# Gated linear attention with a segment memory: key sums of both signs on 128 lanes, denominators inverted once, k weights on a second queue, a new order

## The chip, the cores and the metric

One core of one Trainium2 chip runs the whole kernel. The metric is device time of the program in microseconds (us), lower is better. The engines are TensorE (PE), VectorE (DVE), ScalarE (ACT), GpSimd (POOL) and SyncE (SP); SP only issues DMAs here.

## The reference

The input x has 2048 tokens of 640 numbers, in bf16. Two attentions with 32 heads of 20 numbers each share it, and a gate mixes them:

```
# A: linear attention with softmax features of both signs
q, k, v = split(x @ wqkv)
phi(u)  = concat(softmax(u @ w_phi), softmax(-(u @ w_phi)))   # per head, 40 features
kv = sum over tokens of phi(k) x v ;  z = sum over tokens of phi(k)
o  = (phi(q) @ kv) / (phi(q) @ z + 1e-6);   a = o @ wo
# B: four segments of 512 tokens
per segment: causal softmax attention inside it (a_dot), and a read of a memory M, z (a_mem)
             o = g*a_mem + (1-g)*a_dot;  then M += phi(k) x v, z += sum phi(k)
b = o @ wo_B
out = s*a + (1-s)*b,   s = sigmoid(sum(x * gate_w))
```

## The kernel before

A graph of some 1,380 operations is written down in Python (`setup`, `b_proj`, `b_pair`, `b_out`, `b_mem`, `b_ret`, `a_k`, `a_kv`, `a_fin`, `a_q`, `final`). Three tables, found by a search, fix the rest: `ORDER` lists the operations by number in the order in which each engine's and each queue's instructions are written, `ENGINE` has one digit for each operation that may run on more than one engine, `PLACE` gives each buffer its slot in SBUF or its PSUM banks. An engine runs its instructions in that order and waits on semaphores. SP's DMAs are a queue of the same kind: a DMA that waits for data holds up the ones behind it.

What the change touches:

- `setup` loads x, transposed, and the weights. B's q and k weights come in six pieces each (`stq`, `stk`; L390) and are copied into a padded layout (`WB`, L448).
- `b_out(n)` works on segment n of B. The weighted values and the sums of weights lie in DRAM (`scn`), 32 heads x 21 rows. Four DMAs (`nB<-scn`) bring them back with lanes for features, the sum of each head repeated over its lanes; DVE inverts the sums (`nrec`, L714), and a multiply by them follows (`nmul`, L716).
- `a_k(t)` takes 128 tokens: two exponentials of k @ w_phi with scale +1 and -1 (`kexp`, L738) go to the two planes of the tile E, `Zred` and `Zrec` make the softmax sums, `Anorm` (L748) divides.
- `a_kv(S)` takes four such tiles. On PE, `kv` (L765) multiplies E with v, for each plane with all 128 lanes. For z, the four tiles are added up in a chain into `acc` (`chain`, L787): first on 64 lanes, then a DMA (`accmv`, acc<-acc) moves the sums to the other 64 lanes, and the chain goes on there, for each plane by itself. So it takes 16 adds of 64 lanes x 640 for each S.
- `a_fin` turns `acc` into lanes (L799) and builds `K1` (L809 and L811), the table for the queries; `a_q` and `final` use it. `final(t)` does the output projection of 128 tokens, 20 matmuls (L905), one eviction (`out_ev`, through `evac`, L399 on ACT, L400 on DVE), one DMA.
- A PSUM tile that spans two banks is read with one instruction (`pbanks`).

Of the kernel before, what the change touches and what calls it, by code (L numbers as in the profile page):

```python
# [13 lines left out]
D = 640  # L14
# [21 lines left out]
class Op:  # L36
    __slots__ = ("name", "engs", "fn", "writes", "deps", "tiles", "stream", "idx", "dma", "inc", "key", "val", "vc", "extra", "pos", "part")
# [42 lines left out]
class Graph:  # L80
# [6 lines left out]
    def op(self, engs, name, fn, R=(), W=(), after=(), dma=False, part=128):  # L87
# [17 lines left out]
        o.extra = []  # L105
        self.ops.append(o)
# [49 lines left out]
    def emit(self):  # L156
# [10 lines left out]
        for o in self.order:  # L167
            ds = dict.fromkeys(o.deps)
            if o.stream == "pool" and not o.dma:

                if last is not None and last.part != o.part:
                    ds[last] = None
                last = o
            for t in o.tiles:
                if t in o.writes:
                    for d in t.prev:
                        ds[d] = None
            o.extra = [d for d in ds if d is not o]
            for d in o.extra:
                if not (d.stream == "pe" and o.stream == "pe" and not d.dma):  # L180
                    d.inc = True
# [22 lines left out]
        for o in self.order:  # L204
            st = o.stream
            kn = known[st]
            need = [d for d in o.extra if not (d.stream == "pe" and st == "pe" and not d.dma)]
# [37 lines left out]
class GatedMix(Graph):  # L245
# [34 lines left out]
    def memory(self):  # L280
# [37 lines left out]
        self.onec = fx("onec", [128, 1], BF16)  # L318
# [18 lines left out]
        self.p_z = self.pool("z", 256, 4)  # L337
        self.p_r = self.pool("r", 128, 6)
# [12 lines left out]
        self.scq = [Tile(f"scq{i}", None, None, None) for i in range(2)]  # L351
        for i in range(2):
            self.scr[i].t = nc.dram_tensor(f"scr{i}", [240, 2, LSEG], BF16, kind="Internal").ap()
            self.scn[i].t = nc.dram_tensor(f"scn{i}", [NG, 128, LSEG], BF16, kind="Internal").ap()
            self.scq[i].t = nc.dram_tensor(f"scq{i}", [D, LSEG], BF16, kind="Internal").ap()
# [21 lines left out]
    def pbanks(self, t, n):  # L377

        a = t.t[0]
        assert len(t.t) == 2 and t.t[1] == a + 1  # L380
        return self.ps[:, 512 * a:512 * (a + 2)].rearrange("p (b c) -> p b c", b=2)[:, :, 0:n]
# [23 lines left out]
    def setup(self):  # L405
# [5 lines left out]
        for k in range(2):  # L411
            sl = slice(256 * k, 256 * k + 256)
            self.dma("sp", "x0", xT[:, :, sl], x2d[sl, :], W=[(xT, (0, k))], transpose=True)
        for l, (a, b) in enumerate(((0, 1), (1, 3), (3, NCH))):
            for nm, st in (("B_wq", self.stq), ("B_wk", self.stk)):
                for k, c0, c1 in ((0, 80 * a, 80 * b), (1, 400 + 48 * a, 400 + 48 * b)):
                    self.dma("sp", f"st{k}", st[:, :, c0:c1], wsrc(ins[nm])[:, :, c0:c1], W=[(st, (k, l))], noncontig=True)
        self.dma("sp", "WvB", self.WvB[:, :, 0:D], wsrc(ins["B_wv"]), W=[(self.WvB, "w")])
# [40 lines left out]
        op("dve", "ms", lambda e: e.memset(self.onec[:, :], 1.0), W=[(self.onec, "*")])  # L459
# [23 lines left out]
        bc = lambda a, n: a.rearrange("p (h o) -> p h o", o=1).to_broadcast([128, 4, n])  # L483
        for c in range(NCH):
            gs = lambda j, c=c: eb[:, 2, 4 * c:4 * c + 4] if j == 0 else eb[:, 2, 20 + XH[c]:24 + XH[c]]
            ms = lambda j, c=c: Mg[:, :] if j == 0 else Mx[:, c, XH[c]:XH[c] + 4]
            for j in range(2):
                R = [(eb, "*")] + ([(Mg, "*")] if j == 0 else [(Mx, i) for i in range(4)])
                op("dve", "Mm", lambda e, c=c, j=j, gs=gs, ms=ms: e.tensor_tensor(
                    Mm[:, c, 4 * j:4 * j + 4, 0:DH], bc(ms(j), DH), bc(gs(j), DH), ALU.mult), R=R, W=[(Mm, (c, j, 0))])  # L490
                op("dve", "Mm1", lambda e, c=c, j=j, ms=ms: e.tensor_copy(Mm[:, c, 4 * j:4 * j + 4, DH], ms(j)), R=R, W=[(Mm, (c, j, 1))])
# [87 lines left out]
    def b_mem(self, n):  # L579
# [6 lines left out]
        for b, cs in ((0, (0, 1, 2)), (1, (3, 4))):  # L586
# [16 lines left out]
            else:  # L603
# [3 lines left out]
                R=[(self.M32, b)] + [(self.Mm, (c, j, k)) for c in cs for j in range(2) for k in range(2)], W=[(self.Mz[n % 2], b)])  # L607
# [96 lines left out]
    def b_out(self, n):  # L704

        nB = self.nB[n]
        for dd in range(4):
            self.dma("sp", "nr", lambda dd=dd: nB[32 * dd:32 * dd + 32, :, :],
                     self.scn[n % 2].t.rearrange("g (i r) t -> r (g i) t", r=32)[dd:dd + 24:4].rearrange("c h t -> h c t"),
                     R=[(self.scn[n % 2], "*")], W=[(nB, ("r", dd))])  # L710
        w = 128 if n == 3 else 256
        for q in range(0, LSEG, w):
            qs = list(range(q // 128, (q + w) // 128))
            self.op("dve", "nrec", lambda e, q=q: e.reciprocal(nB[:, NCH, q:q + w], nB[:, NCH, q:q + w]),  # L714
                    R=[(nB, ("r", dd)) for dd in range(4)], W=[(nB, ("d", q))])
            self.op(("dve", "pool"), "nmul", lambda e, q=q: e.tensor_tensor(  # L716
                nB[:, 0:NCH, q:q + w], nB[:, 0:NCH, q:q + w], nB[:, NCH, q:q + w].rearrange("p (o t) -> p o t", o=1).to_broadcast([128, NCH, w]), ALU.mult),
                R=[(nB, ("d", q))] + [(nB, ("r", dd)) for dd in range(4)], W=[(nB, x) for x in qs])
# [11 lines left out]
    def a_k(self, t):  # L730
# [5 lines left out]
        self.op("pe", "pkA", self.tok_proj(pt, t, self.WkA), R=[(self.WkA, ic) for ic in range(NCH)] + self.xk(t), W=[(pt, 0)])  # L736
        for s in range(2):
            self.op("act", "kexp", lambda e, s=s: e.activation(E[:, s, :].rearrange("p (b c) -> p b c", b=2), self.pbanks(pt, 320), ACT.Exp, scale=1.0 - 2.0 * s),  # L738
                    W=[(pt, 0), (E, s)])
# [13 lines left out]
    def a_kv(self, S):  # L753
        ts = [4 * S + i for i in range(4)]
        for s in range(2):
            for b, cs in ((0, (0, 1, 2)), (1, (3, 4))):
                pt = self.pst("kv", 1)
                h0, h1 = CO[cs[0]], (CO + (NHC,))[cs[-1] + 1]

                def mm(e, s=s, pt=pt, cs=cs, h0=h0):  # L760
                    first = True
                    for c in cs:
                        lo, hi = HEADS_OF[c]
                        for t in ts:
                            r = e.matmul(self.pf(pt, 0, DH * (CO[c] - h0), DH * (hi - lo + 1)), lhsT=self.Et[t][:, s, 128 * c:128 * (c + 1)],  # L765
                                         rhs=self.vt[t][:, DH * lo:DH * (hi + 1)], start=first, stop=True, skip_group_check=True)
                            first = False
                    return r
                self.op("pe", f"kv{b}", mm, R=[(self.Et[t], s) for t in ts] + [(self.vt[t], "*") for t in ts], W=[(pt, 0)])
                dst = self.KVa[:, s, h0:h1, :].rearrange("p h d -> p (h d)")  # L770
                src = lambda pt=pt, n=DH * (h1 - h0): self.pf(pt, 0, 0, n)
# [4 lines left out]
        acc = self.acc  # L776
        a, b = (0, 1) if S % 2 == 0 else (1, 0)
        for s in range(2):
            def half(hf, first):
                lo = 64 * hf  # L780
                for k, t in enumerate(ts):
                    src = lambda t=t, s=s, lo=lo: self.Et[t][lo:lo + 64, s, :]
                    R = [(self.Et[t], s)]
                    if first and k == 0:
                        self.op(("dve", "pool"), "chain0", lambda e, src=src, s=s, lo=lo: e.tensor_copy(acc[lo:lo + 64, s, :], src()), R=R, W=[(acc, (hf, s))], part=64 + hf)
                    else:
                        self.op(("dve", "pool"), "chain", lambda e, src=src, s=s, lo=lo: e.tensor_tensor(acc[lo:lo + 64, s, :], acc[lo:lo + 64, s, :], src(), ALU.add),  # L787
                                R=R, W=[(acc, (hf, s))], part=64 + hf)
# [263 lines left out]
```

## Time and profile before

| | |
|---|---|
| median of 3 runs | 303.97 us (302.23 to 304.0) |
| profiled execution, its own time | 304.66 us |
| its span, first to last instruction | 302.9 us |
| granted TensorE clock, mean | 0.994 |
| PE busy | 273.9 us (90%), 2991 matmuls |
| DVE busy | 239.1 us (79%), 407 instructions |
| ACT busy | 242.3 us (80%), 282 |
| POOL busy | 167.2 us (55%), 172 |
| DMA | 36.05 MB, mean 119 GB/s |

Busy time is a sum over instructions. A wait names the instruction that ended it. The chain of waits goes back from the last instruction to what released it, step by step.

### The profile page before, as it was taken

To read this page: it belongs to the slowest core of one execution; us is meant where nothing else is said; L and a number is where in the kernel's file an instruction comes from. 1 tells how busy PE (TensorE), PEld (TensorE's weight loads), DVE (VectorE), ACT (ScalarE), POOL (GpSimd) and SP (SyncE) were. 2 spreads that over 40 slices of the span, in tenths; PEclk is the share of its full clock that TensorE was granted. 3 is DMA by queue.
4 is the path that set the end of the run, shared out by engine and by line. 5 is a ranking of instruction groups with operands and counts; after the bars stand their busy time and mean duration, and the time that the engine had idled before them with its cause. 6 is when DMAs were issued, how large, how long until landed. Compare 5 with 4: busy or idle time off the path is not lost.

```text
span 302.9 us, 7330 instructions
## 1 busy us (share of the span) xinstructions
PE 273.9 (90%) x2991; PEld 165.5 (55%) x3008; DVE 239.1 (79%) x407; ACT 242.3 (80%) x282; POOL 167.2 (55%) x172
## 2 busy tenths in 40 slices
PE   5899999997969889999997898878998999899995
PEld 2676555443646446556744454534474556567773
DVE  4266979789997989998999999898777886674650
ACT  2689898999996859998897798999998998774213
POOL 2355669688375569688832063661395247442091
PEclk9999999999989999999999999999999999999999
DMA  7966989414630142502303575677746956865655
GB/s 130 222 175 124 139 145 185 85 31 104 84 109 2 60 108 56 114 21 71 91 14 70 138 167 132 138 125 117 187 94 155 184 167 137 168 156 150 166 141 99
DMA packets 80786, 36.05 MB, mean 119 GB/s; under 512 B 63952, under 2 KB 78832, under 8 KB 80752
## 3 DMA queue, kind: packets, MB, share of 16 engines
q1 hardware_dynamic: 80656, 35.54, 55.3%
q8 instruction: 24, 0.39, 0.5%
q0 software_dynamic: 96, 0.04, 0.3%
q14 instruction: 10, 0.08, 0.1%
HBM read 12.68 MB, written 11.40 MB: 80 GB/s over the span
## 4 chain that ended last, share of the span: by engine, by line
PE 53%; DVE 23%; DMA 9%; ACT 7%; SPq 4%; issue 2%; POOL 1%; DVEq 0%; ACTq 0%
PE ps L905 14%; PE ps L535 8%; PE ps L726 7%; PE ps L653 5%; DMA oTA<-oA 4%; DVE acc L787 4%; PE ps L696 4%; PE ps L832 4%; ACT exA L664 3%; DMA wqT<-in_A_wqkv_dram 3%; PE ps L877 3%; PE ps L765 2%; DVE z L744 2%; DVE v1B L400 2%; PE ps L556 2%
## 5 line engine op out<-in xcount | busy, mean ns | idle before, releaser
L664 ACT ACTIVATE exA<-ps 128x1024 bf16<-128x1024 f32 x128 | 123.8, 1026 | 17.8 <-PE ps L653 15.7
L666 POOL TENSOR_SCALAR_AFFINE_SELECT exA<-exA 128x1024 bf16<-128x1024 bf16 (+1 forms) x64 | 60.3, 951 | 71.6 <-ACT exA L664 71.2
L535 PE MATMUL ps<-xT,WB 128*128 128x512 bf16 (+1 forms) x239 | 46.3, 335 | 2.5 <-DVE WB L448 0.9
L653 PE MATMUL ps<-qk 20*128 20x256 bf16 (+3 forms) x512 | 31.7, 301 | 9.9 <-DVE v1B L400 2.6
L664 ACT ACTIVATE exC<-ps 128x1024 bf16<-128x1024 f32 x32 | 31.1, 1021 | 5.6 <-PE ps L653 5.5
L535 PEld LDWEIGHTS ps<-xT,WB 128*128 128x128 bf16 x250 | 22.6, 98 | 18.8 <-issue 2.2
L748 POOL TENSOR_TENSOR E<-E,z 128x640 bf16<-128x640 bf16 x22 | 29.2, 1336 | 5.1 <-DVE z L746 4.8
L787 DVE TENSOR_TENSOR acc<-acc,E 64x640 bf16<-64x640 bf16 x48 | 30.5, 654 | 0.9 <-DMA acc<-acc 0.3
L653 PEld LDWEIGHTS ps<-qk 20*128 20x128 bf16 x512 | 9.2, 92 | 31.4 <-ACT exA L664 6.4
L666 POOL TENSOR_SCALAR_AFFINE_SELECT exC<-exC 128x1024 bf16<-128x1024 bf16 x16 | 18.1, 1137 | 14.3 <-ACT exC L664 14.3
L556 PE MATMUL ps<-WvB,xT 128*128 128x320 bf16 x80 | 23.3, 310 | 2.5 <-DVE qk L400 1.4
L744 DVE TENSOR_REDUCE z<-E 128x64 f32<-128x1280 bf16 x16 | 23.5, 1471 | 2.4 <-ACT E L738 2.4
L832 PE MATMUL ps<-xT,WqA 128*128 128x512 bf16 x94 | 23.3, 380 | 2.0 <-DVE oA L886 1.4
L726 PE MATMUL ps<-WvA,xT 128*128 128x320 bf16 x160 | 24.2, 305 | 0.7 <-ACT exC L664 0.4
L696 PE MATMUL ps<-exA,v1B 128*32 128x384 bf16 (+2 forms) x384 | 22.3, 311 | 2.6 <-DVE WqA L400 1.4
L905 PE MATMUL ps<-Wo,nB 128*128 128x320 bf16 x160 | 24.1, 300 | 0.3 <-ACT exA L664 0.3
L787 POOL TENSOR_TENSOR acc<-acc,E 64x640 bf16<-64x640 bf16 x14 | 20.8, 1491 | 6.1 <-DVE acc L787 2.9
L726 PE MATMUL ps<-WkA,xT 128*128 128x320 bf16 x160 | 24.1, 299 | 0.1
L905 PE MATMUL ps<-Wo,oTA 128*128 128x320 bf16 x160 | 24.1, 299 | 0.0
L738 ACT ACTIVATE E<-ps 128x640 bf16<-128x640 f32 x32 | 22.3, 711 | 1.7 <-DVE acc L787 1.0
L557 PE MATMUL ps<-WvB,xT 128*128 128x321 bf16 x80 | 23.4, 310 | 0.0
L839 ACT ACTIVATE ET<-ps 128x1024 bf16<-128x1024 f32 (+1 forms) x24 | 20.9, 885 | 2.7 <-DVE acc L787 1.6
(119 smaller groups left out, 491.3 us busy)
## 6 DMA issues: line engine op xcount, KB each, us to landing
scn<-nT SPq DMA_DIRECT2D x32, 128.0 KB, 1.8
nB<-scn SPq DMA_DIRECT2D x16, 192.0 KB, 3.4
scq<-rr SPq DMA_DIRECT2D x16, 160.0 KB, 3.0
sp<-scq SPq DMA_DIRECT2D x4, 640.0 KB
out_dram<-out SPq DMA_DIRECT2D x16, 160.0 KB, 2.0
scr<-qk SPq DMA_DIRECT2D x16, 120.0 KB
qk<-scr SPq DMA_DIRECT2D x16, 120.0 KB
WvB<-in_B_wv_dram SPq DMA_DIRECT2D x1, 800.0 KB
```

Source lines behind the costliest of these rows:

```text
L535: r = e.matmul(self.pf(pt, w, h * N, N), lhsT=WB[:, w, kc, 128 * c:128 * (c + 1)], rhs=xT[:, kc, LSEG * n + h * N:LSEG * n + (h + 1) * N], ...
L556: e.matmul(self.pf(pt, 0, 0, 320), lhsT=l, rhs=self.WvB[:, kc, 0:320], start=(kc == 0), stop=(kc == 4))
L653: r = e.matmul(self.pf(pts[i // 2], i % 2, c0, N), lhsT=qk[32 * i:32 * i + DH, g, 1, 128 * j:128 * (j + 1)], rhs=qk[32 * i:32 * i + DH, g, ...
L664: self.op("act", "exp", lambda e, p=p: e.activation(view(p), self.pbanks(pts[p], 512), ACT.Exp, scale=scale), W=[(pts[p], 0), (t, (key, p))])
L666: self.op("pool", "mask" + str(len(pat)), lambda e: e.affine_select(mv(), mv(), pattern=pat, compare_op=ALU.is_ge, fill=0.0, base=0, chann ...
L696: r = e.matmul(self.ps[32 * i:32 * i + 32, 512 * pt.t[0] + 128 * j:512 * pt.t[0] + 512], lhsT=vt[:, v0:v0 + 32], rhs=src(j, i), start=(j = ...
L726: r = e.matmul(self.pf(pt, b, 0, 320), lhsT=l, rhs=W[:, kc, 320 * b:320 * b + 320], start=(kc == 0), stop=(kc == 4))
L744: self.op("dve", "Zred", lambda e: e.tensor_reduce(z[:, :, :].rearrange("p s h -> p (s h)"), E[:, :, :].rearrange("p s (h d) -> p (s h) d" ...
L748: self.op(("pool", "dve"), "Anorm", lambda e, s=s: e.tensor_tensor(Ev(s), Ev(s), z[:, s, :].rearrange("p (h o) -> p h o", o=1).to_broadcas ...
L787: self.op(("dve", "pool"), "chain", lambda e, src=src, s=s, lo=lo: e.tensor_tensor(acc[lo:lo + 64, s, :], acc[lo:lo + 64, s, :], src(), AL ...
L832: r = e.matmul(self.pf(pt, k, 0, LSEG), lhsT=self.WqA[:, kc, 128 * c:128 * (c + 1)], rhs=xT[:, kc, LSEG * S:LSEG * (S + 1)], start=(kc == ...
L905: r = e.matmul(self.pf(pt, b, 0, 320), lhsT=lhs(c), rhs=self.Wo[:, NCH * k + c, 320 * b:320 * b + 320], start=(first and c == 0), stop=(no ...
```

## The change

- **Signs.** `kexp` takes its scale from a tile `sg` with one number for each lane. Plane p of E now has exp(+) on one half of the lanes and exp(-) on the other, so that one add on 128 lanes serves both signs. `a_kv` adds the four tiles of one plane, moves both halves with two DMAs to the other half of the other plane, and adds the four tiles of that plane: 8 adds of 128 x 640 for each S.
- **kv.** The product is done in halves of 64 lanes, which go to the two halves of PE's rows (`tile_position`) and to two banks. Four kv operations for each S before (two planes, two groups of chunks), four after (two halves `p0` and `p1`, two groups), each with twice the matmuls. `fence` makes PE wait for its own first half before the second, which writes the same banks from the other rows.
- **Sums of weights.** For segments 0 to 2, four DMAs read the sums alone into `den` (`dr`), one reciprocal of 128 x 128 inverts them (`drec`), one DMA writes them to DRAM (`dw`), four read them back repeated (`dn`), and `nmul` waits for these. The last segment is as before.
- **Weights.** The six k pieces and `WvB` are issued by ACT, the rest by SP. The second piece of x comes ahead of the later q pieces.
- **Small ones.** The masks `Mm` of the first four heads of all chunks are made by two instructions, not ten; `K1`'s sums for both signs by 5, not 10 (`K1z2`); the sums' matmul has 5 steps, not 10.
- **End.** The last four tiles are projected, evicted and written in halves of 320 columns.
- **Tables.** `ORDER`, `ENGINE` and `PLACE` are new throughout.

Counted off from the tables, what runs where (before, after):

| operation | before | after |
|---|---|---|
| chain, copies included | DVE 49, POOL 15 (64 lanes) | DVE 22, POOL 10 (128 lanes) |
| nrec and drec | DVE 10 | DVE 4 + 3 |
| Anorm | POOL 22, DVE 10 | POOL 26, DVE 6 |
| Esc, nmul, Mz on DVE / POOL | 15 / 13 | 14 / 14 |
| qk, nT, vA, v evictions on DVE / ACT | 53 / 31 | 62 / 22 |
| WB copies on ACT / DVE / POOL | 9 / 7 / 4 | 3 / 7 / 10 |
| out evictions on ACT / DVE | 10 / 6 | 6 + 7 halves / 6 + 1 half |
| DMAs dr, dw, dn on SP | 0 | 12, 3, 12 |

On ACT the order of the start is: k pieces 1 to 3, a WB copy of piece 3's columns, k piece 4, a WB copy of piece 4's, k pieces 5 and 6, the first exponential, `WvB`. On DVE, `drec1` follows the sums of S = 2, then come `Zrec` of tiles 12 and 13, `Anorm` of tile 13, the first plane of the last chain, `nmul1.0`, and the second plane. On SP the two last `accmv` stand behind the `dn` of segment 1. After the last products of the queries PE has 14 projections of one half (A's or B's) of 128 tokens left, as many as before.

```
-        for s in range(2):
-            self.op("act", "kexp", ... scale=1.0 - 2.0 * s), W=[(pt, 0), (E, s)])
+        for s in range(2):
+            self.op("act", "kexp", ... scale=self.sg[:, s:s + 1]), R=[(self.sg, (k, s)) for k in range(2)], W=[(pt, 0), (E, s)])

+                        for t in ts:
+                            for k in range(2):
+                                r = e.matmul(self.pf(pt, pl ^ k, DH * (CO[c] - h0), DH * (hi - lo + 1)), lhsT=self.Et[t][64 * k:64 * k + 64, pl, 128 * c:128 * (c + 1)],
+                                             rhs=self.vt[t][64 * k:64 * k + 64, DH * lo:DH * (hi + 1)], start=(pl == 0 and k not in first), stop=True,
+                                             tile_position=(64 * k, 0), skip_group_check=True)
+            halves[1].fence = (halves[0],)
...
+        def plane(p, first):
+            for k, t in enumerate(ts):
...
+                    self.op(("dve", "pool"), "chain", lambda e, src=src: e.tensor_tensor(acc[:, p, :], acc[:, p, :], src(), ALU.add), R=R, W=[(acc, (p, 0)), (acc, (p, 1))])
         a, b = (0, 1) if S % 2 == 0 else (1, 0)
+        plane(a, S == 0)
+        for k in range(2):
+            self.dma("sp", "accmv", acc[64 - 64 * k:128 - 64 * k, b, :], acc[64 * k:64 * k + 64, a, :], R=[(acc, (a, k))], W=[(acc, (b, 1 - k))])
+        plane(b, False)
...
+        if not last:
+            den = self.den
+            for dd in range(4):
+                self.dma("sp", "dr", lambda dd=dd: den[32 * dd:32 * dd + 32, :], scn.t.rearrange("g (i r) t -> r (g i) t", r=32)[DH, :, 128 * dd:128 * dd + 128],
+                         R=[(scn, "*")], W=[(den, dd)])
+            self.op("dve", "drec", lambda e: e.reciprocal(den[:, :], den[:, :]), W=[(den, dd) for dd in range(4)])
+            self.dma("sp", "dw", scd.t[:, :], lambda: den[:, :], R=[(den, dd) for dd in range(4)], W=[(scd, "*")])
...
+            for q, nm, st in (("sp", "B_wq", self.stq), ("act", "B_wk", self.stk)):
                 for k, c0, c1 in ((0, 80 * a, 80 * b), (1, 400 + 48 * a, 400 + 48 * b)):
+                    self.dma(q, f"st{k}", st[:, :, c0:c1], wsrc(ins[nm])[:, :, c0:c1], W=[(st, (k, l))], noncontig=True)
```

## Rows read from the trace of the kernel before

**Rows 1.** Busy time of each engine by stretch; times from the span's start.

```profile
core 0: us, PE busy (x) PEld busy (x) DVE busy (x) ACT busy (x) POOL busy (x), PEclk, DMA share, GB/s
0.00:3.09 3.09, 0.00 (x1) 0.01 (x1) 1.87 (x7) 1.28 (x1) 1.62 (x7) 1.00 0.27 61
3.09:12.43 9.34, 8.40 (x47) 4.49 (x47) 2.71 (x10) 2.90 (x6) 2.11 (x7) 1.00 1.07 199
12.43:280.74 268.31, 246.44 (x2807) 147.59 (x2825) 225.95 (x379) 233.34 (x270) 155.04 (x152) 0.99 0.54 115
```

**Rows 2.** Waits: engine, line, releaser; us in total, times, longest.

```profile
PE ps L653 <- DVE v1B L400: 2.6, 4, 1.1
...
PE ps L653 <- DVE aM L634: 0.2, 1, 0.2
DVE nB L714 <- DMA nB<-scn: 3.4, 2, 2.7
```

**Rows 3.** The chain of waits: start, us, what.

```profile
145.41 1.49 DVE KVa L775 x3
...
163.93 3.32 DMA acc<-acc
...
169.56 0.50 DVE acc L787
...
280.74 19.03 PE ps L905 x140
299.80 0.79 ACT out L399
```

**Rows 4.** Groups by line and form: busy us, mean ns; idle before and releasers.

```profile
L787 DVE TENSOR_TENSOR acc<-acc,E 64x640 bf16<-64x640 bf16 x48 | 30.5, 654 | 0.9 <-DMA acc<-acc 0.3
L748 DVE TENSOR_TENSOR E<-E,z 128x640 bf16<-128x640 bf16 x10 | 9.2, 932 | 0.1
L400 DVE CAST nT<-ps 128x512 bf16<-128x512 f32 x20 | 13.4, 679 | 2.8 <-PE ps L696 2.3 <-DMA scn<-nT 0.5
L400 DVE CAST qk<-ps 128x1024 bf16<-128x1024 f32 x11 | 13.4, 1215 | 3.0 <-PE ps L535 3.0
L714 DVE RECIPROCAL nB<-nB 128x256 bf16<-128x256 bf16 x6 | 10.5, 1744 | 0.7 <-DMA nB<-scn 0.7
...
L399 ACT ACTIVATE out<-ps,omg 128x640 bf16<-128x640 f32 x10 | 7.9, 795 | 17.5 <-PE ps L905 17.5
L399 ACT ACTIVATE vA<-ps 128x640 bf16<-128x640 f32 x8 | 5.6, 719 | 0.4 <-PE ps L726 0.4
L714 DVE RECIPROCAL nB<-nB 128x128 bf16<-128x128 bf16 x4 | 3.6, 932 | 2.7 <-DMA nB<-scn 2.7
L640 DVE TENSOR_TENSOR nB<-nB,aT 128x640 bf16<-128x640 bf16 x6 | 3.1, 516 | 5.7 <-DMA aT<-aM 5.6
L809 DVE TENSOR_SCALAR KV<-Mk,zf 128x7 bf16<-128x7 bf16 x8 | 3.0, 382 | 0.0
```

**Rows 5.** The chain of waits, pieces on PE: start, us, what.

```profile
68.82 1.19 PE ps L535 x5
...
140.53 0.33 PE ps L653 x8
...
144.01 1.37 PE ps L765 x20
...
174.36 0.95 PE ps L594 x24
```

**Rows 6.** Timeline of SP's queue at the start: start, us, what is issued.

```profile
9.99 1.77 SPq L390 DMA_DIRECT2D stk<-in_B_wk_dram  x2
```

**Rows 7.** DMA issues: count, KB each, median us to landing.

```profile
scn<-nT SPq DMA_DIRECT2D x32, 128.0 KB, 1.8
nB<-scn SPq DMA_DIRECT2D x16, 192.0 KB, 3.4
...
stk<-in_B_wk_dram SPq DMA_DIRECT2D x2, 120.0 KB, 3.8
```

More of the change, by code (lines that the diff above doesn't have):

```diff
@@ L36 @@
 class Op:
-    __slots__ = ("name", "engs", "fn", "writes", "deps", "tiles", "stream", "idx", "dma", "inc", "key", "val", "vc", "extra", "pos", "part")
+    __slots__ = ("name", "engs", "fn", "writes", "deps", "tiles", "stream", "idx", "dma", "inc", "key", "val", "vc", "extra", "pos", "part", "fence")
 class Tile:
@@ L206, in emit @@
             kn = known[st]
-            need = [d for d in o.extra if not (d.stream == "pe" and st == "pe" and not d.dma)]
+            need = [d for d in o.extra if not (d.stream == "pe" and st == "pe" and not d.dma) or d in o.fence]
             need.sort(key=lambda d: -d.pos)
@@ L351, in memory @@
         self.scq = [Tile(f"scq{i}", None, None, None) for i in range(2)]
+        self.scd = [Tile(f"scd{i}", None, None, None) for i in range(2)]
         for i in range(2):
@@ new lines, in b_out @@
+        for dd in range(4):
+            self.dma("sp", "nr", lambda dd=dd: nB[32 * dd:32 * dd + 32, 0:nc, :],
+                     scn.t.rearrange("g (i r) t -> r (g i) t", r=32)[dd:dd + 4 * nc:4].rearrange("c h t -> h c t"),
+                     R=[(scn, "*")], W=[(nB, ("r", dd))])
+        if not last:
+            for dd in range(4):
+                self.dma("sp", "dn", lambda dd=dd: nB[32 * dd:32 * dd + 32, NCH, :].rearrange("p (k t) -> p k t", k=4), scd.t.rearrange("(k h) t -> h k t", k=4),
+                         R=[(scd, "*")], W=[(nB, ("d", dd))])
@@ L712, in b_out @@
+        w = 128 if last else 256
         for q in range(0, LSEG, w):
             qs = list(range(q // 128, (q + w) // 128))
[L714 to L715 removed]
+            if last:
+                self.op("dve", "nrec", lambda e, q=q: e.reciprocal(nB[:, NCH, q:q + w], nB[:, NCH, q:q + w]),
+                        R=[(nB, ("r", dd)) for dd in range(4)], W=[(nB, ("d", q))])
@@ L754, in a_kv, with mm @@
         ts = [4 * S + i for i in range(4)]
-        for s in range(2):
[L756 to L761, printed above, removed]
+        for b, cs in ((0, (0, 1, 2)), (1, (3, 4))):
+            pt = self.pst("kv", 2)
+            h0, h1 = CO[cs[0]], (CO + (NHC,))[cs[-1] + 1]
+            halves = []
+            for pl in range(2):
+                def mm(e, pt=pt, cs=cs, h0=h0, pl=pl):
+                    first = set()
                     for c in cs:
```

152 lines of the change are left out of this document (79 added, 73 removed), and 100 rows, old and new, of tables (ORDER, PLACE).

## The prediction

> **What bounds the kernel now.** I read the busy time of stretches first, then the waits of TensorE (PE), then the chain of waits, then the price of each kind of instruction.
>
> The stretches [rows 1] show where PE stands still. PE does nothing in the first 3.09 us but is close to full up to 12.43 us. From there to 280.74 us it is busy 246.44 of 268.31 us, so 21.87 us are idle; VectorE (DVE) is busy 225.95 us of that stretch, 84%, ScalarE (ACT) 233.34. No engine is free, and PE is the fullest.
>
> The waits of PE say who ended that idle time. The rows that name DVE run from 2.6 us down to 0.2 us [rows 2]; there are 17 of them without the one that starts the warm-up, and they add up to 15.4 us, of which 0.9 us is a weight copy of the start. So some 14.5 us of the 21.87 end with a DVE instruction: DVE is what keeps PE waiting.
>
> The chain of waits [rows 3] shows the same at two places. From about 145 to 170 us it hardly leaves DVE: sums of keys (acc, line 787), then the move of their lanes, DMA acc<-acc, 3.32 us. And the end is PE alone: 140 matmuls of the output projection in 19.03 us, then one eviction of 0.79 us. Nothing waits there but work, so PE time saved or lost earlier comes out at the end.
>
> **The change part by part.** The engine table and the order table of the diff, counted off against the order in which the code makes its operations, say which engine gets what (front section).
>
> *DVE.* The adds of the key sums fall from 49 to 22 on DVE. A 64-lane one took 654 ns in the mean [rows 4]. A 128-lane add of 640 elements isn't in this loop; the nearest rows are the 64-lane one and line 640, a 128-lane add of the same length, 516 ns. I take 654: 27 fewer are -17.7 us, and with the first copy, which was a short one, -17.2. Six reciprocals of 128x256 at 1744 ns give way to three of 128x128; the 128x128 ones of the last segment took 932 ns [rows 4]: -10.5 +2.8 = -7.7. The merged masks and K1 columns are 13 fewer small instructions, at 382 ns at most -5.0, but the merged ones are longer: -3. Of the broadcast multiplies (normalising, scaling) DVE gets five fewer net, 932 ns each: -4.7. Evictions go the other way: 4 more of qk at 1215 ns, 4 more of nT at 679 ns [rows 4], one more net of v and vA between these: +8.4. Sum -24.2 us, of which 23 in the long stretch, where DVE goes from 226 to 203 us busy and from 42 to 65 us idle.
>
> *ACT and GpSimd (POOL).* ACT loses those evictions and six weight copies. But the exponentials of the keys get their sign as a scale per lane: 32 of them. An ACT eviction with a scale per lane took 795 ns (out), one without 719 (vA) [rows 4], so +0.076 each, +2.4 us. Over all ACT has some 7 us less, POOL some 5 us more (five fewer sums, four more normalisings, two more scalings). Both stay below PE; I count nothing for either.
>
> *What DVE's relief is worth (term C).* That DVE does less only helps where PE waits for it. If a wait shortens with the queue in front of it, busy over idle, it goes from 226/42 to 203/65, to 0.58 of what it was: 14.5 x 0.42 = -6.0 us, an estimate. Bounds: 0 (other waits take their place) and -14.5 (all of them gone).
>
> *The key-value product on PE (term B).* 160 matmuls of 128 rows become 320 of 64 rows, in pairs on the two halves of the array. Before, 20 took 1.37 us [rows 5], 68.5 ns each, 11.0 us in all. Two halves at once are not in this trace. Quarters at once are: a QK burst, 8 matmuls on four row groups with 512 columns for each, took 0.33 us, while 5 matmuls of 512 columns on the whole array took 1.19, 0.24 each [rows 5]. So row groups do run together, and to go into that arrangement and out again costs some 0.09 us: 16 halves x 0.09 = +1.5. The doubled weight loads could show as well: the shortest spacing of load and matmul in the rows is 24 in 0.95 us, 39.6 ns [rows 5], which makes 320 of them 12.7 us, +1.7. And if two halves didn't overlap at all it would be 320 x 68.5 = 21.9, +11. Below nothing is excluded, since no matmul streams fewer columns. I take +2.0, near the QK row; PE has no cover for it.
> The Trainium skill speaks against this part (TensorEngine Tiling, Key Properties): "Changing tiling mode (not just tile) drains the TensorE", but the same list has tiles load and multiply in parallel. By that list B would be the drains alone, +1.5 and a sum 0.5 lower; by the spacing row it would be +3.2. The QK row agrees with the list for quarters, and no row here shows halves.
>
> The wait that PE puts on itself between the two halves of a product (they write the same bank from other rows) has other matmuls between in most of the order; nothing.
>
> *The start (term A).* The k weights and WvB leave SP's queue for ACT's. SP issued the last pair of k pieces at 9.99 us [rows 6], and such a piece lands 3.8 us after its issue [rows 7]. ACT can issue the first three at once, in the 3 us in which the DMA engines are 0.27 busy [rows 1]. But ACT's queue is in order: the order puts the fourth piece behind a weight copy that waits for the third, and the last two behind one that waits for the fourth. Two landings in a row from about 2.5 us on reach 10 us, and the last lands at 14 to 15: no earlier than now. From 3.09 to 12.43 us the DMA engines are full (share 1.07). SP in turn comes to x and wkT sooner. Bounds -2.2 (the idle DMA time of the first 3 us is won whole) and +1.5 (the last k pieces late); -0.7.
> The Trainium skill (DMA: Bandwidth & Descriptors, Issuing engines are not separate DMA queues) says that issuing from a second engine saves only the time of issuing. By that A is 0 and the sum 0.7 higher; the full share agrees with it, the 0.27 of the first stretch leaves room.
>
> *Denominators.* Three times, four small reads of the denominators, a reciprocal, one write and four reads back: 27 more issues on SP, and three new waits in a row. What is queued behind them: on DVE the reciprocal of segment 1 stands right behind its reads in the order, with the normalising of tiles 12 and 13 after it; then comes the multiply of segment 1, behind the reads back, and only after it the second half of the last key sums. On SP the last acc<-acc move stands behind the reads back, which wait for the write. This is in the neck of 145 to 170 us. A scn write landed in 1.8 us, an nB read in 3.4 [rows 7]. If the queue is ahead by that much it costs nothing. I take nothing, since DVE stood on reads of nB only twice before, 3.4 us in all [rows 2], and keep 0 to 8.6 us (below) for the range.
>
> *The end (term D).* The last eviction is one of half a tile: 0.79 us [rows 3] becomes about 0.5; the four last tiles have twice the output DMAs, and SP issues them one behind another. -0.3, between -0.8 and +0.6.
>
> **Sum.** The profiled execution took 304.66 us (span 302.90, 1.76 around it). 304.66 - 0.7 (A) + 2.0 (B) - 6.0 (C) - 0.3 (D) = 299.7. It stood 0.7 above the median of the runs, 303.97, so as a median 299.0.
>
> **Rivals.**
> *The relief isn't used* (C = 0): the work that DVE gets rid of was not what PE waited for in that order, or a 128-lane add takes twice a 64-lane one. For it: ACT is as full as DVE. Against: 15.4 us of waits name DVE. 305.0.
> *All waits on DVE go* (C = -14.5): the order is searched anew and can put every eviction in time. For it: DVE falls to 76% in the stretch; against: ACT and POOL have hardly any more room, and the long chains stay. 290.5.
> *The neck stalls* (slower). DVE waits at the reciprocal of segment 1 for its reads, 3.4 us, and at the multiply for the write, 1.8, and a read back, 3.4 [rows 7]: 8.6 us, and the issues between them, in which the last key sums, and so K1 and the queries behind them, stand. 299.0 + 8.6 = 307.6. It makes the kernel slower by over 1% from 8.0 us on, which it reaches where each read is issued only as DVE comes to it. For it: the order has the last three of these reads right ahead of the reciprocal. Against: those two waits are all there was of the kind.
>
> **How the numbers follow.** What a measurement here can tell from no change is about 1%, 3.0 us. Forecast 0.46 (its own range 295.5 to 302), relief not used 0.23, all waits gone 0.17, neck 0.14. Faster by over 1% (below 300.9): 0.17 and most of 0.46, 0.57. Slower (above 307.0): the neck and a little of the unused relief, 0.15. Within: 0.28. The range leaves out the lower half of the best case and most of the neck: 290.5 to 307.5, which holds A, B and D at their bounds but for the case of no overlap.
>
> **What would show it.** DVE at 215 us busy in the new page; line of the key sums with 21 adds near 650 ns on DVE; PE's waits on DVE at 8 to 9 us in all; the kv matmuls taking some 13 us of PE; exponentials of keys near 790 ns; PE again the end of the chain for some 19 us. The forecast is wrong if the adds on 128 lanes cost about 1.3 us, if PE's idle time stays near 22 us with other releasers, or if DVE shows waits of several us on DMA den or nB around 150 us.

## The result, and the profile after

The changed kernel took 295.19 us (median of 4 runs, 294.42 to 297.45) against 303.75 us for the kernel before on the same chip: a ratio of 0.974, 95% interval 0.969 to 0.979. The profiled execution took 295.64 us, its span is 293.6 us, and the mean granted clock of PE was 1.0. Where the median of a run below includes executions that the comparison leaves out, its ratio is the number to read.

The first and the fourth part of the new page: busy time of the engines, and the chain that ended last by engine; the last line is that chain in the kernel before.

```profile
PE 277.9 (95%) x3163; PEld 164.1 (56%) x3163; DVE 220.8 (75%) x376; ACT 235.7 (80%) x270; POOL 172.2 (59%) x178
...
PE 47%; ACT 22%; DMA 12%; DVE 10%; SPq 3%; POOL 3%; issue 2%; ACTq 0%
...
PE 53%; DVE 23%; DMA 9%; ACT 7%; SPq 4%; issue 2%; POOL 1%; DVEq 0%; ACTq 0%
```

DVE has 18.3 us less work than before and went from second place in the chain (23% before) to fourth. ACT has taken its place. Who ended PE's waits (engine, line, releaser; us in total, times, longest), to be read beside [rows 2]:

```profile
PE ps L668 <- ACT exA L679: 1.5, 5, 0.5
PE ps L550 <- DMA xT<-in_A_x_dram: 1.3, 1, 1.3
PE ps L445 <- DVE onec L471: 1.3, 1, 1.3
PE ps L944 <- DVE oA L923: 1.2, 1, 1.2
PE ps L550 <- ACT exA L679: 0.9, 3, 0.5
...
PE ps L550 <- DVE nT L406: 0.2, 1, 0.2
```

Without the warm-up's 1.3 us (L445), all rows that name DVE add up to 2.5 us; before they were 15.4. Those that name ACT rose from 4.4 to 6.3 us. In the repetition shown below the same sums are 4.2 and 8.0. All rows together went from 24.3 to 12.2 us, and to 15.3 in the repetition; the span is 9.3 and 9.2 us shorter. So the fall of the waits, 12.1 and 9.0 us, is large enough for the gain. It isn't all that changed: the granted clock rose from 0.994 to 1.0, which over 302.9 us is at most 1.8 us, an estimate. (PE's busy time can't be compared across the two pages: 17 of 3008 matmuls have no record in the one before, none of 3163 in this one, and 22 in the repetition.)

Groups of DVE and ACT by line and form (busy us, mean ns; idle before), beside [rows 4]:

```profile
L406 DVE CAST qk<-ps 128x1024 bf16<-128x1024 f32 x15 | 18.2, 1215 | 4.1 <-PE ps L550 4.0
...
L822 DVE TENSOR_TENSOR acc<-acc,E 128x640 bf16<-128x640 bf16 x22 | 11.7, 532 | 0.6 <-DMA acc<-acc 0.4
...
L779 DVE TENSOR_TENSOR E<-E,z 128x640 bf16<-128x640 bf16 x6 | 8.7, 1458 | 0.0
...
L746 DVE TENSOR_TENSOR nB<-nB 128x1280 bf16<-128x1280 bf16 x3 | 3.2, 1056 | 0.8 <-DMA nB<-scd 0.8
...
L730 DVE RECIPROCAL den<-den 128x128 bf16<-128x128 bf16 x3 | 2.8, 942 | 0.0
...
L769 ACT ACTIVATE E<-ps,sg 128x640 bf16<-128x640 f32 x32 | 24.8, 814 | 2.5 <-PE ps L756 1.9
```

Key sums: from 30.5 to 11.7 us; an add on 128 lanes took 532 ns in the mean, one on 64 lanes 654. Six normalisings on DVE take as long as ten did, because each is slower (1458 against 932 ns); the last section comes back to this.

Two places of the chain of waits (start, us, what), beside [rows 3] and [rows 5]: the neck and the end.

```profile
144.51 1.36 PE ps L799 x40
...
158.23 2.58 DMA nB<-scd
160.82 0.02 issue
160.84 0.82 DVE nB L746
...
278.04 12.92 PE ps L944 x95
290.96 0.02 issue
290.98 0.53 ACT out L405
```

The key-value product takes 1.36 us for 40 half matmuls, where 20 whole ones took 1.37. The neck shows the feared wait, DVE's multiply behind a read back of `scd`; the row of that multiply (L746) has it at 0.8 us.

### The profile page after: what moved, and what is told of

It is laid out like the page before. It is cut to its first block, busy times and chain, and to the rows that moved or that the text cites. A ratio compares the mean times of both kernels' runs of the same rounds, so it can differ in the third digit from the quotient of the medians.

```text
span 293.6 us, 7651 instructions
## 1 busy us (share of the span) xinstructions
PE 277.9 (95%) x3163; PEld 164.1 (56%) x3163; DVE 220.8 (75%) x376; ACT 235.7 (80%) x270; POOL 172.2 (59%) x178
## 4 chain that ended last, share of the span: by engine, by line
PE 47%; ACT 22%; DMA 12%; DVE 10%; SPq 3%; POOL 3%; issue 2%; ACTq 0%
ACT exA L679 11%; PE ps L550 10%; PE ps L944 10%; PE ps L756 7%; ACT E L769 5%; PE ps L869 4%; PE ps L668 4%; DMA sp<-scq 4%; PE ps L711 3%; ACT exC L679 3%; SPq L397 3%; DMA oTA<-oA 3%; PE ps L914 2%; DMA xT<-in_A_x_dram 2%; ACT ET L876 2%
## 5 line engine op out<-in xcount | busy, mean ns | idle before, releaser
L679 ACT ACTIVATE exA<-ps 128x1024 bf16<-128x1024 f32 x128 | 122.6, 1034 | 15.0 <-PE ps L668 14.5
L550 PE MATMUL ps<-xT,WB 128*128 128x512 bf16 (+1 forms) x250 | 50.4, 344 | 3.1 <-DMA xT<-in_A_x_dram 1.3
L779 POOL TENSOR_TENSOR E<-E,z 128x640 bf16<-128x640 bf16 x26 | 33.9, 1312 | 16.1 <-DVE z L777 9.0
L550 PEld LDWEIGHTS ps<-xT,WB 128*128 128x128 bf16 x250 | 22.7, 100 | 23.6 <-issue 5.3
L668 PE MATMUL ps<-qk 20*128 20x384 bf16 (+3 forms) x512 | 31.7, 301 | 2.5 <-ACT exA L679 1.5
L769 ACT ACTIVATE E<-ps,sg 128x640 bf16<-128x640 f32 x32 | 24.8, 814 | 2.5 <-PE ps L756 1.9
L869 PE MATMUL ps<-xT,WqA 128*128 128x512 bf16 x100 | 24.3, 380 | 1.1 <-ACT exA L679 0.5
L756 PE MATMUL ps<-WvA,xT 128*128 128x320 bf16 x160 | 24.3, 300 | 0.3 <-ACT E L769 0.3
L405 ACT ACTIVATE out<-ps,omg 128x320 bf16<-128x320 f32 (+1 forms) x13 | 8.2, 651 | 20.2 <-PE ps L944 20.2
L756 PE MATMUL ps<-WkA,xT 128*128 128x320 bf16 x160 | 23.8, 300 | 0.4 <-ACT exA L679 0.4
L711 PE MATMUL ps<-exA,v1B 128*32 128x384 bf16 (+2 forms) x384 | 22.6, 311 | 1.1 <-POOL exA L681 0.8
L681 POOL TENSOR_SCALAR_AFFINE_SELECT exC<-exC 128x1024 bf16<-128x1024 bf16 x16 | 19.7, 1233 | 5.9 <-ACT exC L679 5.9
L572 PE MATMUL ps<-WvB,xT 128*128 128x321 bf16 x80 | 22.5, 300 | 0.0
L668 PEld LDWEIGHTS ps<-qk 20*128 20x128 bf16 x512 | 9.0, 92 | 23.7 <-issue 7.7
L746 POOL TENSOR_TENSOR nB<-nB 128x1280 bf16<-128x1280 bf16 (+1 forms) x6 | 12.0, 2000 | 17.2 <-DVE nB L744 17.2
```

Of the source, the lines that this page charges most:

```text
L550: r = e.matmul(self.pf(pt, w, h * N, N), lhsT=WB[:, w, kc, 128 * c:128 * (c + 1)], rhs=xT[:, kc, LSEG * n + h * N:LSEG * n + (h + 1) * N], ...
L668: r = e.matmul(self.pf(pts[i // 2], i % 2, c0, N), lhsT=qk[32 * i:32 * i + DH, g, 1, 128 * j:128 * (j + 1)], rhs=qk[32 * i:32 * i + DH, g, ...
L679: self.op("act", "exp", lambda e, p=p: e.activation(view(p), self.pbanks(pts[p], 512), ACT.Exp, scale=scale), W=[(pts[p], 0), (t, (key, p))])
L681: self.op("pool", "mask" + str(len(pat)), lambda e: e.affine_select(mv(), mv(), pattern=pat, compare_op=ALU.is_ge, fill=0.0, base=0, chann ...
L711: r = e.matmul(self.ps[32 * i:32 * i + 32, 512 * pt.t[0] + 128 * j:512 * pt.t[0] + 512], lhsT=vt[:, v0:v0 + 32], rhs=src(j, i), start=(j = ...
L756: r = e.matmul(self.pf(pt, b, 0, 320), lhsT=l, rhs=W[:, kc, 320 * b:320 * b + 320], start=(kc == 0), stop=(kc == 4))
```

## The experiments

Each run has a ratio to the kernel before on its chip, with its 95% interval; where I turn a difference of ratios into us I multiply it by 304. Twelve runs follow, one of them the changed kernel again; the edits are shortened to the lines that matter. The first six ask what the relief of DVE is worth (term C), and whether it is the relief or the new order.

**1. The old amount of DVE work in the new order.** Each addition of the key sums on DVE in three pieces of the lanes, or in two.

```
-    e.tensor_tensor(acc[:, p, :], acc[:, p, :], src(), ALU.add)
+    for l, h in (((0, 64), (64, 96), (96, 128)) if o.stream == "dve" else ((0, 128),)):
+        r = e.tensor_tensor(acc[l:h, p, :], acc[l:h, p, :], self.Et[t][l:h, p, :], ALU.add)
```

> The changed kernel, but each addition to the key sums on VectorE is made in three pieces (lanes 0 to 63, 64 to 95, 96 to 127) instead of one of 128 lanes. By the 0.532 us that one addition took in the changed kernel, two more pieces for some 21 additions add 22 to 25 us to VectorE's 220.8 us busy: its amount of work is again that of the kernel before (245), in the new order. Theory 1 (the gain is VectorE's relief, and the new order needs it): VectorE's waits come back on TensorE, 302 to 307 us, a ratio to the kernel before of 0.995 to 1.01. Theory 2 (the gain is the newly searched order, whatever the work is): 295 to 297 us, ratio below 0.98.

> The changed kernel, but each addition to the key sums on VectorE is made as two additions of 64 lanes: some 11 to 14 us more on VectorE, half of what it was relieved of. Theory 1 (relief, in proportion): 299 to 301 us, ratio 0.985 to 0.99. Theory 2 (order): 295 to 296 us, ratio 0.975. If relief counts only beyond a point (slack used up), less than half of the loss of the run with three pieces.

Three pieces: 331.73 us, ratio 1.0883 (1.0838 to 1.0929), DVE busy 257.1 us. Two pieces: 317.99 us, 1.0443 (1.0415 to 1.0471), DVE busy 244.1. Both theories fell: the first asked for at most 307. So did the thought that relief counts only beyond a point: two pieces cost 0.62 of what three cost, not less than half. The new order doesn't only need the relief; with as much DVE work as before, or a little more, it is far slower than the kernel before. Waits of PE in the run with two pieces, then one of its windows of 100 us (busy time of each engine, granted clock, DMA share, GB/s):

```profile
PE ps L668 <- DVE KVa L812: 3.7, 1, 3.7
PE ps L571 <- DVE qk L406: 3.7, 1, 3.7
PE ps L756 <- DVE qk L406: 2.5, 1, 2.5
```

```profile
100.00:200.00 100.00, 87.28 (x985) 48.46 (x984) 86.38 (x130) 76.43 (x87) 57.61 (x51) 0.93 0.34 75
```

The longest waits aren't on the key sums at all, but on evictions (qk) and the adding up of the product (KVa) that are queued behind them on DVE. All waits add up to 31.0 us, 18.8 more than in the changed kernel, and PE is busy for 4.8 us longer: after waits of 3.7, 1.8 and 3.7 us in this window its matmuls ran at the lower of its two clock levels (1.2 instead of 2.4 GHz) for a time (granted clock 0.93 here, 1.00 in the other windows). 18.8 + 4.8 = 23.6; the span is 23.7 us longer.

**2. Less DVE work in the old order.** In the kernel before, every second addition of the key sums on DVE takes 8 columns, and so does the second reciprocal of segments 0 to 2.

```
+    w = 8 if o.stream == "dve" and k % 2 else D
+    return e.tensor_tensor(acc[lo:lo + 64, s, 0:w], acc[lo:lo + 64, s, 0:w], self.Et[t][lo:lo + 64, s, 0:w], ALU.add)
...
+    v = 8 if q and n < 3 else w
```

> The kernel before in its own order, with VectorE relieved in place: every second addition to the key sums on VectorE works on 8 columns instead of 640, and the second reciprocal of the denominators of segments 0 to 2 on 8 columns instead of 256 (these sums and reciprocals are left out). Some 25 x 0.6 + 3 x 1.65 = 20 us less on VectorE. Theory 1 (relief): TensorE's waits on VectorE shrink in the old order too, 291 to 297 us, ratio 0.96 to 0.975. Theory 2 (the order): 302 to 304 us, ratio 0.995 to 1.

299.91 us, 0.9855 (0.983 to 0.988). DVE was relieved of 13.8 us (225.3 busy), and 4.4 came back: 0.32 us for each us. PE's waits on DVE fell by 4.9 us, to 13.6 with the warm-up's 3.1. So relief alone does work, but for less than theory 1 asked, which had counted on 20 us of relief.

**3. More DVE work in the old order.** Every second addition in two pieces of 32 lanes.

```
+    n = 32 if o.stream == "dve" and k % 2 else 64
+    for l in range(lo, lo + 64, n):
+        r = e.tensor_tensor(acc[l:l + n, s, :], acc[l:l + n, s, :], self.Et[t][l:l + n, s, :], ALU.add)
```

> The kernel before in its own order, with every second addition to the key sums on VectorE made as two additions of 32 lanes: some 24 more instructions of 0.5 to 0.8 us, 12 to 18 us more on VectorE. In the changed kernel 23 us more cost 22.8 us. Theory 3 (an order fitted to its durations pays for added VectorE work in full, whichever order it is, and gets back only a part of what is taken away): 316 to 322 us, ratio 1.04 to 1.06. Theory 4 (only the new order is that tight; the old one has slack, as its 0.31 us per us of relief lets one think): 308 to 310 us, ratio 1.015 to 1.02.

323.49 us, 1.0632 (1.060 to 1.0664), DVE busy 256.8: 17.7 us of work cost 19.2 us. This is theory 3, a little beyond its range; the old order is just as tight. PE's waits on DVE grew by 11.6 us, and PE was busy for 7.5 us longer at a granted clock of 0.974 instead of 0.994 (17 matmuls lack a record in both traces). So part of the price of added work is the clock.

**4. Less DVE work in the new order, and the changed kernel again.** All additions of the key sums on DVE with 8 columns.

```
+    w = 8 if o.stream == "dve" else D
+    return e.tensor_tensor(acc[:, p, 0:w], acc[:, p, 0:w], self.Et[t][:, p, 0:w], ALU.add)
```

> The changed kernel with every addition to the key sums on VectorE on 8 columns instead of 640 (most of the key sums are left out): some 22 x 0.45 = 10 us less on VectorE. Theory 3 (a third of what is taken away comes back, in the new order as in the old): 291 to 293 us, ratio 0.96 to 0.965. Theory 5 (TensorE no longer waits for VectorE, so more relief is worth nothing): 294.5 to 295.5, ratio 0.974. If the relation is one to one in both directions: 285, ratio 0.94.

> The changed kernel again, unchanged, on the same chip as these runs, as the measure for the runs of single parts: 295.2 us, ratio 0.974. The single parts undone lay at 0.966 (key-value product whole), 0.9651 (constant sign), 0.9757 (tail whole) and 0.9777 (one queue); where they differ from this ratio by less than the intervals, nothing follows.

The changed kernel again: 295.64 us, 0.9728 (0.9689 to 0.9767). With 7.2 us less on DVE: 295.34, 0.9706 (0.968 to 0.9733). That is 0.7 us less and not told apart from none, as theory 5 said; a third of 7.2 us would be 2.4. Its reason isn't quite right: waits on DVE remain, 4.6 us here and 4.2 in the repetition without the warm-up, but by this run the key sums aren't what they hang on. The repetition ran on the chip of runs 1 to 4; of the runs below, the one-queue, constant-sign and tail runs and the old denominators ran on another, where the kernel before took 304.95 instead of 304.31 us. So only the ratios compare.

The two orders side by side; the us are the ratio times 304:

| DVE busy | order before | order after |
|---|---|---|
| 214.5 | | 295.1 |
| 221.7 | | 295.7 |
| 225.3 | 299.6 | |
| 239.1 | 304 | |
| 244.1 | | 317.5 |
| 256.8 / 257.1 | 323.2 | 330.8 |

Each order has a knee somewhere near the amount of work that it was found for; so few points don't place it. Above it a us of DVE costs about a us (old 1.08, new 0.97 and 1.03); below it a us gave back a third in the old order and 0.1, not told apart from nothing, in the new one. At equal work of 257 us the new order is 7.6 us slower, so it isn't the better one by itself. That it was fitted to the shorter instructions is how I read this; no run searched an order anew. This work was added or taken away at the key sums (in run 2 also at reciprocals); that another place would give the same slopes is not shown.

**5. The single parts.** Term A undone: `("act", "B_wk", ...)` and `"act", "WvB"` back to `"sp"`.

> The changed kernel with the k weights and WvB issued by SyncE again, at the same places of the order (term A undone). Prediction: 0.7 us slower, 295.9 us. Rival (the transfers are bound by the DMA engines, whoever issues them): no difference, 295.2. Second rival (ScalarE's queue in order holds the last k pieces back, the first exponential at 13.07 us against 12.44 before): 0.5 to 1 us faster, 294.5.

298.04 us, 0.9777 (0.974 to 0.9814): 1.5 us slower than the repetition, the intervals overlap. The trace points the same way. First exponential of this run, then of the changed kernel (ACT's timeline; idle before and releaser); then the first two windows of this run and the first of the changed kernel:

```profile
14.64 1.02 ACT L679 ACTIVATE exA<-ps 128x1024 bf16<-128x1024 f32 x1 [4.40 <-PE ps L668]
...
13.07 1.02 ACT L679 ACTIVATE exA<-ps 128x1024 bf16<-128x1024 f32 x1 [2.18 <-PE ps L668]
```

```profile
0.00:10.00 10.00, 5.60 (x17) 2.07 (x18) 2.43 (x12) 1.98 (x3) 3.35 (x13) 0.92 0.87 151
10.00:20.00 10.00, 9.71 (x86) 7.18 (x85) 5.45 (x17) 4.75 (x6) 6.00 (x18) 0.91 1.06 229
...
0.00:10.00 10.00, 7.47 (x23) 3.23 (x24) 2.95 (x14) 1.82 (x2) 3.70 (x15) 1.00 1.00 163
```

PE was busy for 5.60 us of the first ten instead of 7.47, and the DMA engines 0.87 instead of 1.00. Part of the later exponential may be the lower clock of these windows (0.92 and 0.91; 1.00 in the changed kernel), and not every execution had a lower clock: three of this run's six had a granted clock of 1.0 and took 296.9 to 297.9 us, the others 298.2 to 299.3.

Term B: the key-value product as 160 matmuls of 128 rows, each plane to its own bank, with no fence. This mixes the two signs.

```
-                            for k in range(2):
-                                r = e.matmul(self.pf(pt, pl ^ k, ...), lhsT=self.Et[t][64 * k:64 * k + 64, pl, ...], ..., tile_position=(64 * k, 0), ...)
+                            r = e.matmul(self.pf(pt, pl, ...), lhsT=self.Et[t][:, pl, ...], rhs=self.vt[t][:, ...], ...)
-            halves[1].fence = (halves[0],)
```

> The changed kernel with the key-value product as 160 matmuls of 128 rows instead of 320 of 64 rows in pairs, and no wait between the two planes (the product then mixes the two signs). The prediction's term B (switching the array's arrangement, 2.0 us of TensorE): 293 to 293.5 us. Rival (the halves run fully side by side and nothing is paid for switching): 295 us, no difference beyond 0.5 us. Second rival (the wait between the planes stands on TensorE, 0.6 us in the trace): 294.5 us.

Ratio 0.966 (0.9612 to 0.9707), 293.7 us by the ratio: some 2 us faster than the repetition, with overlapping intervals. PE's timeline of two groups of products, in this run and then in the changed kernel:

```profile
140.82 1.03 PE L550 MATMUL ps<-xT,WB 128*128 128x512 bf16 x4
141.69 1.41 PE L798 MATMUL ps<-vA,E 128*128 128x140 bf16 x20
143.03 0.40 PE L668 MATMUL ps<-qk 20*128 20x128 bf16 x8
143.36 1.42 PE L798 MATMUL ps<-vA,E 128*128 128x140 bf16 x20
144.62 0.57 PE L756 MATMUL ps<-WkA,xT 128*128 128x320 bf16 x3
```

```profile
141.80 1.03 PE L550 MATMUL ps<-xT,WB 128*128 128x512 bf16 x4
142.76 1.42 PE L799 MATMUL ps<-vA,E 64*128 64x140 bf16 x40
144.11 0.40 PE L668 MATMUL ps<-qk 20*128 20x128 bf16 x8
144.44 1.42 PE L799 MATMUL ps<-vA,E 64*128 64x140 bf16 x40
145.80 1.94 PE L756 MATMUL ps<-WkA,xT 128*128 128x320 bf16 x13
```

From the start of the first product to the QK burst it is 1.34 us here and 1.35 us there. So the halves run side by side, and the 320 loads don't show. The switching does, at the borders with matmuls of the whole array. From the four matmuls of L550 to the product it is 0.87 us here and 0.96 there, and from the second product to L756 1.26 and 1.36: some 0.09 to 0.10 us for each change between whole array and halves. A border with a QK burst costs the halves nothing extra, since QK, on quarters, is a change for whole products too. In the changed kernel's trace the product stands in ten stretches; of their 20 borders 6 are with matmuls of the whole array, the other 14 with QK bursts or the matmuls of L711, which use a part of the array. That makes 0.6 us in all, an estimate. The fence's own waits, 0.6 us in 3, are on weight loads (PEld); no stretch is over 0.01 us longer than one of whole products between the same neighbours. The other 1.4 of the 2 us, if they are real, have no place in the traces that I could find.

The sign of the key exponentials as a constant; both halves of the lanes then get one sign.

> The changed kernel with the sign of the key exponentials as a constant instead of one value per lane (both halves of the lanes then get the same sign, so the sums and the product mix up differently). ScalarE loses 32 x 0.10 = 3.3 us. If ScalarE is now what TensorE waits for (waits that end with ScalarE are 6.6 us): 293 to 294.5 us. If TensorE is bound by its own work: 295.

The row of these exponentials in this run, beside the one of the changed kernel further up:

```profile
L769 ACT ACTIVATE E<-ps 128x640 bf16<-128x640 f32 x32 | 22.1, 731 | 2.7 <-PE ps L756 2.2
```

293.54 us, 0.9651 (0.96 to 0.9702), 2.3 us faster than the repetition. The exponentials took 731 ns instead of 815, and ACT was busy for 233.6 us instead of 236.0; the gain is as large as these 2.4 us. The intervals just overlap. At a granted clock of 1.0 four executions took 292.5 to 293.6 us, five of the repetition 294.6 to 296.5. This is what a kernel would do whose PE now waits for ACT; that it is ACT's load, and not that the keys come earlier, is not shown.

Term D undone: the last four tiles in one piece, `parts = ((0, 1),)`, their operations at the place of the later half.

> The changed kernel with the last four tiles of the output in one piece each, as before (term D undone), their products at the place of the later half. Prediction: 0.3 us slower, 295.5. By the two traces (2.65 us after the last matmul against 3.1): 0.45 us slower. Rival (twice the output transfers cost as much as the shorter eviction wins): no difference.

297.50 us, 0.9757 (0.9709 to 0.9806): not told apart from 0.9728. In the traces the end after the last matmul is 3.1 us in this run and 2.7 in the changed kernel, so D is worth 0.4 us there.

**6. The denominators.** As before the change, with two reciprocals right ahead of the multiplies; and the same with these on 8 columns (`v = w if last else 8`; the sums then stay uninverted). The order is otherwise the changed kernel's.

```
-        if not last:
-            ... dr, drec, dw
-        if not last:
-            ... dn
-            if last:
-                self.op("dve", "nrec", ...)
+            self.op("dve", "nrec", ...)
```

> The changed kernel with the denominators of segments 0 to 2 as in the kernel before: read with the weights and inverted by two 128x256 reciprocals on VectorE each, right ahead of each multiply; no small reads, write and reads back. VectorE gets 6 x 1.74 - 3 x 0.94 = 7.6 us more work. If the small reads cost their queue nothing (prediction): slower by VectorE's share of the relief, 7.6 of 24 us, that is +1 to +3 us, 296 to 298. If the chain of transfers holds the neck up (the rival): faster, 294 or less.

> The changed kernel without the small reads, the write and the reads back of the denominators of segments 0 to 2, and with their reciprocals on 8 columns only (these denominators stay uninverted): VectorE has 3 us less, SyncE 27 issues less, and the three waits in a row are gone. If that chain is hidden but for its 0.8 us in the neck (the trace of the changed kernel): 293.5 to 294.5 us, ratio 0.97. If its issues hold other transfers back along the whole kernel: 291 or less, ratio below 0.96.

Old denominators: 311.74 us, 1.0204 (1.0155 to 1.0254), 14.5 us slower than the repetition at 234.9 us of DVE: 13.2 us more work (7.7 of it the reciprocals), above the knee. Without inverting: 299.08 us, 0.983 (0.9787 to 0.9872), 3.1 us slower although transfers and waits were taken away. Both expectations were wrong, and the second trace shows what happens. Its POOL waits, then POOL's timeline (last the same multiply in the changed kernel) and PE's:

```profile
POOL nB L734 <- DVE nB L732: 23.6, 5, 13.5
```

```profile
182.52 2.60 POOL L734 TENSOR_TENSOR nB<-nB 128x1280 bf16<-128x1280 bf16 x1 [3.96 <-DVE nB L732]
185.08 1.89 POOL L620 TENSOR_TENSOR Mz<-M,Mm 128x504 bf16<-128x504 f32 x1
...
179.09 2.60 POOL L746 TENSOR_TENSOR nB<-nB 128x1280 bf16<-128x1280 bf16 x1
```

```profile
187.11 0.55 PE L640 MATMUL ps<-Mz,pq 128*128 128x84 bf16 x10 [1.94 <-POOL Mz L620]
...
188.07 0.47 PE L572 MATMUL ps<-WvB,xT 128*128 128x321 bf16 x1
188.34 0.47 PE L571 MATMUL ps<-WvB,xT 128*128 128x320 bf16 x1
```

Such waits are 17.3 us in 3 in the repetition of the changed kernel; here they are 23.6 us in 5. A reciprocal of 0.19 us, put right ahead of its multiply, has to queue on DVE; POOL's multiply waits 3.96 us for it, the memory's product `Mz` behind it comes late, PE stands for 1.94 us, and soon after that its matmuls start every 0.27 us instead of 0.14, the lower of the two clock levels (1.2 instead of 2.4 GHz). In the changed kernel that multiply runs from 179.09 us. So by this trace the early reciprocal of `den` buys more than its 7.6 us of work: it takes DVE out of the way between the sums and POOL's multiply. There is a rival: DVE was not relieved at all here, 224.0 us busy against 221.7, since some of its instructions with two inputs ran longer (the 14 columns of `K1` 931 ns in the mean instead of 603; the last section shows why), and 2.3 us at the slope of the table would make most of the 3.1 us. The two aren't told apart. These runs have the reciprocal at another place as well as without the transfers; what the transfers alone cost was not measured apart, and the 0.8 us of the trace stand.

## Why the prediction was right, and by how much it missed

The forecast was 299.0 us, the range 290.5 to 307.5; measured 295.19. The direction and the reason, relief of DVE, were right: PE's waits on DVE are what fell. The miss is 3.8 us. By the runs and traces some 1.4 of it lie in B, 0.8 in A and 0.1 in D; that leaves 1.5 for C and for what no run tells apart, which is less than the 3 us that a measurement here can tell.

*C (-6.0), right in its mechanism, its size shown only in part.* The rule busy over idle was made for relief in a given order, and there it did well: for run 2 it gives 4.3 us, an estimate, where 4.4 were measured, and for run 3 12 us, where the waits on DVE grew by 11.6 (the clock, which it leaves out, came on top). Carried linearly, run 2's price makes 5.8 us of the 18.3 us of the change, an estimate, next to the 6.0. What the step left out is that the order is new as well. All but 2.5 us of the waits on DVE went, 12.9 us, and not the 6.0 that the rule takes off. Some of it came back as waits on ACT (1.9 us more) and at the start (1.3 us on x). Of the 8.6 us measured, 5.8 for the relief, 1.5 for A and 0.4 for D, less 0.6 for B, leave 1.5 us, which may be the order's; no run shows it, since none has the changed instructions in the old order. By itself the order is not the better one: at 257 us of DVE work it is the slower, by 7.6 us.

*B (+2.0), mis-sized: 0.6.* The price of a change of arrangement was about right: 0.09 us was taken for a QK burst, in and out; the traces show 0.09 to 0.10 each way. (The row had 1.19 us for 5 matmuls of the whole array, 0.24 each; they start 0.216 us apart, and the rest is the change at their end.) The count was wrong: 16 halves were priced, but only 6 borders are with the whole array. The spacing of loads didn't show: 34 ns for each half matmul, against the 39.6 that I took for the shortest. The Trainium skill (TensorEngine Tiling (Array Packing), Key Properties) says that a change of tiling mode drains the engine and that tiles load and multiply in parallel; the trace agrees with both, with 0.09 to 0.10 us for a change and 1.35 us for 40 halves where 20 whole ones took 1.34. The sign named in the prediction, 13 us of kv matmuls, came out at 13.2 by luck: by the same measure, busy time of the group, the product took 13.8 us before, and not the 11.0 that the sign was built on.

*A (-0.7), right in sign.* 1.5 us by the ratios, unresolved, 1.6 us by the first exponential, the clock included. I argued that two landings in a row on ACT's queue would eat it up. But the gain is on the other side: with one queue the DMA engines are less busy and PE starts later. This prices the second queue in the new order alone. Against the kernel before, where the first exponential started at 12.44 us, both are late (13.07 and 14.64). The Trainium skill's rule (DMA: Bandwidth & Descriptors, Issuing engines are not separate DMA queues), that a second issuer saves only the issuing, isn't contradicted: SP issued a pair of k pieces in 1.77 us [rows 6], so the six pieces are some 5 us of issuing, an estimate.

*D (-0.3).* 0.4 us by the traces. *Denominators (0).* The mechanism of the neck was there, with 0.8 of the 8.6 us; the queue was ahead of it.

*DVE's sum* came out at -18.3 instead of -24.2. The adds helped (532 instead of 654 ns). The broadcast multiplies, forecast at -4.7, gave nothing: 20.9 us before and 21.2 after (E, ET, nB and Mz), the normalisings among them at 1458 instead of 932 ns. ACT at -6.6 (forecast -7; the scale per lane cost 3.3 us instead of 2.4) and POOL at +5.0 came as forecast. PE's idle time of 21.87 us was read too high: 18 of the 2825 matmuls of that stretch have no record, at 0.216 us each up to 3.9 us.

*Rivals.* "All waits on DVE go" came nearest in its mechanism, but not in its price, since ACT is next in line. "Relief not used" is refuted by run 2, the stall of the neck by its 0.8 us.

## What to carry to other kernels

In two orders of this kernel, each found by search for given durations, a us added to the busy in-order engine cost about a full us, part of it through the clock, and a us taken away paid a third or next to nothing. So price a saving and a new order together, and try the saving alone in the old order before you credit either. When most waits on one engine are gone, look at the engine that is next: here a constant instead of a scale per lane on ACT brought 2.3 us and 7.2 us less of DVE's key sums 0.7, both at or below the edge of what the runs tell apart. And look for the price of a change of PE's arrangement where it borders on matmuls of the whole array, not beside work that changes it anyway.

## What was not expected of the hardware

DVE's additions and multiplies with two inputs in SBUF stretch beside some of POOL's instructions. DVE and POOL in the changed kernel (timelines):

```profile
157.49 2.58 DVE L822 TENSOR_TENSOR acc<-acc,E 128x640 bf16<-128x640 bf16 x5
...
173.53 0.40 DVE L844 TENSOR_TENSOR KV<-Mk,zf 128x14 bf16<-128x14 bf16 x3
...
175.85 1.41 DVE L844 TENSOR_TENSOR KV<-Mk,zf 128x14 bf16<-128x14 bf16 x1
```

```profile
161.70 0.63 POOL L681 TENSOR_SCALAR_AFFINE_SELECT exA<-exA 128x512 bf16<-128x512 bf16 x1 [5.62 <-ACT exA L679]
...
175.54 1.64 POOL L655 TENSOR_TENSOR nB<-nB,aT 128x640 bf16<-128x640 bf16 x1
```

The same instruction of 14 columns takes 0.13 us while POOL is idle and 1.41 us when it starts behind a POOL add; it ends as that one does (177.26 and 177.18). The Trainium skill (SBUF — State Buffer, Who interferes with whom) says that such a DVE instruction reads its second input through an interface shared with POOL, under an exclusive lock, and that the order of issue decides who blocks; the trace agrees. It fits the 1458 ns of the normalisings too: four of the six ran beside a normalising that POOL had begun and took 1.44 to 1.90 us, the other two 0.81. In run 1 it is part of the price. There eight additions of 64 lanes from 179.21 us on took 8.25 us beside a working POOL, ten from 171.07 us on 5.40 us with POOL idle for most of it (timelines of the run with two pieces):

```profile
171.07 5.40 DVE L826 TENSOR_TENSOR acc<-acc,E 64x640 bf16<-64x640 bf16 x10
...
179.21 8.25 DVE L826 TENSOR_TENSOR acc<-acc,E 64x640 bf16<-64x640 bf16 x8
```

In the changed kernel five of the last sums run from 157.49 us on, inside the 5.62 us in which POOL is idle, at 0.52 us each.
